# Order and pairing of the DFT pieces in an adaLN block with an S4D convolution and a token MLP

## The chip, the cores and the metric

The kernel runs on one core of a Trainium2 chip. A core has five engines with a row of instructions each: TensorE (PE, with its weight loads as PEld), VectorE (DVE), ScalarE (ACT), GpSimd (POOL) and SyncE (SP), which here only issues DMAs. The metric is the device time of the core in microseconds, lower is better; of several runs the median counts.

## The reference

An adaLN block over x of 2048 tokens by 448 channels. Six vectors (sa, ca, ga, sb, cb, gb) come from a small condition vector c. All in 32-bit floats:

```python
h = _layernorm(x, axis=-1) * (1 + ca) + sa
x = x + ga * _A_ref(h, ...)
h = _layernorm(x, axis=-1) * (1 + cb) + sb
x = x + gb * _B_ref(h, ...)
```

`_A_ref` is an S4D convolution along the tokens. Its kernel is a sum of 256 complex exponentials per channel, and the convolution goes through an FFT of twice the length:

```python
P = jnp.exp((A * dt[:, None])[:, :, None] * pos[None, None, :])
K = 2.0 * jnp.einsum("dn,dnl->dl", C, P).real
y = jnp.fft.irfft(Uf * Kf[None, :, :], L2)[:, :, :L]
```

`_B_ref` is a layer norm and a two-layer MLP with gelu over the tokens (2048 to 1792 to 2048), shared by the channels.

## The kernel before, in words

**Kernel generation.** The 448 channels go through in 28 groups of 16, each in two halves of 128 exponentials: 56 steps s. Eight steps make a batch. At its start stands a *window* (`window`), in which ScalarE computes magnitudes with the exponential table (L612); then come eight steps with the sine table. A step consists of: the phase product xe, xg on PE for the next step (L601, `st_phase`); six activations on ScalarE (L642 to L647); the two products G on GpSimd (L649, L650); the four products E on VectorE (L651 to L655); 64 small matmuls kg of the step before on PE (L676, `st_kgen`); and every second step a copy ks by ScalarE (L690). The tiles of the phase product are free for the next one when E has read them. Every four steps PE forms y from two groups (L714, `st_s1`), which is the first stage of the DFT of K; two PSUM buffers go to it, and ScalarE copies them to yk (L720).

**Pieces.** The convolution is done in a two-stage DFT. Its second stage is cut into 32 pieces of 224 columns: pieces 0 to 15 are the first half of the channels, 16 to 31 the second. A piece n consists of:
- `pc_load`: a load of u, the transformed input (224 KB), on SP (L739), and for n below 16 of its DFT tables si;
- `pc_s2`: the forward product kx, 8 matmuls on PE (L770) into one buffer of the PSUM pool `pms` (three buffers, shared with y and, for n below 16, with vv);
- `pc_mul`: the products zx and zy with u on VectorE (L778), and two sums z on engines that the caller names (L780, L781);
- `pc_tables`: for n above 16 the second table bt, made of the first by a negated and a plain copy (L759, L760); it has three buffers;
- `pc_inv`: the way back vv, 8 matmuls on PE (L795), two PSUM buffers; for n of 16 and above out of a pool of four, `pxs`;
- `pc_out`: two copies vt by ScalarE (L801) and a store to v_d in DRAM on SP (L803).

The tables of the first half are kept in the buffer yks[0], which its data no longer need (`pc_keep`, L750).

From step 33 on the first 16 pieces are woven into the generation steps by `piece`. It is called once a step (L1111), and in a window at three of its eight places. A call with `go` loads, issues kx and puts `pc_mul` into the list `dve`; where a piece was open before, it issues its way back and puts `pc_out` into the list `act`. These lists are emptied in the next step at fixed places (`flush`): `dve` between the second and third product E, `act` after the six activations. In the steps, `go` holds at odd s; at even s the call only brings the way back.

**Last stage.** When all of K is there, the pieces 16 to 31 run in one loop: in each turn load and kx of piece n, its products, one sum on GpSimd and one on VectorE, bt of piece n+1, and the way back of piece n-2. Then the token MLP: it reads v_d back as vt (L1198), makes the second stage of the way back as y (L1218), normalizes, and multiplies (acc, L1190 to L1192; o, L1324 to L1326). Its weights come through `WeightStream` with three raw buffers of 448 KB (L182); xt are rows of x (L1134, `x_pair`).

**What sets the order.** On PE, ACT, DVE and POOL the order is that in which the code is written. On SP a scheduler sets it, but for sections entered with `manual_schedule` for SP: in the last stage from the turn of piece 28 on (`last`). There the first w and the first xt go out in the turn of piece 29, and the second w after the loop.

Of the kernel before, what the change touches and what calls it, by code (L numbers as in the profile page):

```python
# [11 lines left out]
F32 = mybir.dt.float32  # L12
F32R = mybir.dt.float32r
BF16 = mybir.dt.bfloat16
AF = mybir.ActivationFunctionType
ALU = mybir.AluOpType
# [6 lines left out]
P = 128  # L23
# [193 lines left out]
def tile_adaln_s4d_mixer(ctx, tc, i, out):  # L217
# [20 lines left out]
    with ExitStack() as es:  # L238
# [496 lines left out]
        def pc_load(n):  # L735
            c, p = divmod(n, NP)
            u = fp.tile([P, 2, DC], F32, tag="u", name="u", bufs=4)
            rows = us_d[c, 2 * p : 2 * p + 2].rearrange("k (q c) d -> (k q) (c d)", c=2)
            nc.sync.dma_start(u.rearrange("p c d -> p (c d)"), rows)  # L739
            if c:  # L740
                w = kept(p)
            else:
                w = fp.tile([P, 4 * P], F32, tag="si", name="si", bufs=4)
                nc.sync.dma_start(w, si[:, p])
            pl[n] = u, w
            pt[n] = w[:, 2 * P : 3 * P], None if c else w[:, 3 * P : 4 * P]
# [5 lines left out]
        def pc_tables(n):  # L752

            real, h = pt[n][0], P // 2
            if n == NP:
                pt[n] = real, t0[:, 1]
                return
            imag = fp.tile([P, P], F32, tag="bt", name="bt", bufs=3)
            G.tensor_scalar(imag[:, 0:h], real[:, h:P], -1.0, None, ALU.mult)  # L759
            G.tensor_copy(imag[:, h:P], real[:, 0:h])  # L760
            pt[n] = real, imag

        def pc_s2(n):
            c, p = divmod(n, NP)
            k1 = yks[c][:, 2 * p : 2 * p + 2]
            pk[n] = pms.tile([P, 2, DC], F32, tag="ms", name="kx")
            for a in range(2):
                for k in range(2):
                    m = k * P + a * P // 2
                    T.matmul(  # L770
                        pk[n][64 * k : 64 * k + 64, a], pl[n][1][:, m : m + 64], k1[:, k], start=True, stop=True
                    )

        def pc_mul(n, e0, e1):
            u = pl.pop(n)[0]
            x, y, z = (fp.tile([P, 2, DC], F32, tag=t, name=t, bufs=b) for t, b in (("zx", 2), ("zy", 2), ("z", 3)))
            for j, t in enumerate((x, y)):
                V.tensor_tensor(t, pk[n], u[:, j : j + 1].to_broadcast([P, 2, DC]), ALU.mult)  # L778
            pk.pop(n)
            e0.tensor_tensor(z[:, 0], x[:, 0], y[:, 1], ALU.subtract)  # L780
            e1.tensor_tensor(z[:, 1], x[:, 1], y[:, 0], ALU.add)  # L781
            pz[n] = z, y

        def pc_inv(n):
            c, p = divmod(n, NP)
            pv[n] = [(pxs if c else pms).tile([P, DC], F32, tag="ms", name="vv") for _ in range(2)]
            z, y = pz.pop(n)
            terms = [(t, z[:, j], 2) for j, t in enumerate(pt.pop(n))]
            if p == 0:
                terms.append((t0[:, 0], y[:, 1], 1))  # L790
            for j, (t, zz, ks) in enumerate(terms):
                for k in range(ks):
                    r = slice(64 * k, 64 * k + 64)
                    last = j == len(terms) - 1 or (k == 1 and j == 1)
                    T.matmul(pv[n][k], t[r], zz[r], start=j == 0, stop=last)  # L795
# [150 lines left out]
                if k is not None:  # L946
                    f(k)

        def piece(go, eng=None):

            due = pieces[1] < pieces[0]
            if go:
                n = pieces[0]
                if n + 3 < 2 * NP:
                    pc_load(n + 3)
                pc_s2(n)
                if n:
                    pc_keep(n - 1)
                dve.append(partial(pc_mul, n, eng or G, eng or G))
                pieces[0] += 1  # L960
            if due:
                n = pieces[1]
                pc_inv(n)
                act.append(partial(pc_out, n))
                pieces[1] += 1
# [67 lines left out]
        for s in range(tail):  # L1033
            if s == 32:
                early.close()
                fp = es.enter_context(tc.tile_pool(name="fp", bufs=2, reuse_waits="tile"))
                m2p.append(right("m2l", BATCH - 3))
                yks[1] = fp.tile([P, 32, DC], F32, name="yk1", bufs=1)
                for n in range(3):
                    pc_load(n)  # L1040
                t0 = fp.tile([P, 2, P], F32, name="t0", bufs=1)
                nc.sync.dma_start(t0, i["T0"].rearrange("p (j m) -> p j m", j=2))
            if s % 2 == 0 and 0 < s and s // 2 + 2 < NG:
                load(s // 2 + 2, False)
            if s == 8:
                first.close()
            if s in late:
                late[s]()
            if s < NHALF and s % BATCH == 0:
                window(s)  # L1050
                if s == 0:
                    gp_ = right("gp", 3)
            if s % BATCH == 4:
                for g in range(s // 2 + 2, min(s // 2 + 6, NG)):
                    load(g, True)

            def between():
                flush(dve)
                if 2 <= s < BATCH:
                    for r in range(2 * s, 2 * s + 2):  # L1060
                        u_stats(r)
                if s < len(pace):
                    more(pace[s])

            mellow()
            if s >= NHALF:
                flush(dve)
                mellow()
            else:
                if s < 32 and s % BATCH > 1:  # L1070
                    st_kgen(s - 2)
                if (s + 1) % BATCH:
                    st_phase(s + 1)
                elif s + 1 < NHALF:
                    st_exponents(s + 1)

                if s > 32 and s % BATCH:
                    st_kgen(s - 1)
                st_step(s, between)
            flush(act)  # L1080
            if s == NHALF:
                st_kgen(s - 1)


            if s < 2:
                x_load(4 + 4 * s, 4 + 4 * s, G)
            free = s > 7 and not st_s1(s % BATCH == BATCH - 1)
            if s + 2 < 32 and (s + 2) % BATCH > 1:
                st_mag2(s + 2)

            if 1 < s < 8:
                modulation(s // 2, s % 2)
            if s == 7:
                par_load(2)

            if 8 <= s < 16 and free:
                some(u_rows, rows, 2 if s % 2 else 3)
            if s == 12:
                par_load(3)
            if s == 16:  # L1100
                spec.close()
                up = early.enter_context(tc.tile_pool(name="up", bufs=3, reuse_waits="tile"))
                for n in range(4):
                    u_load(n)
            if 17 <= s < 32 and free:
                some(u_cols, cols, 2 if s < 24 else 3)
            if s == 31:
                flush(dve)
                flush(act)
            if s > 32:  # L1110
                piece(pieces[0] < NP and (s % 2 == 1 or s >= NHALF))  # L1111
            if s == 34:

                for t in (ft, b1, b2):
                    V.memset(t, 0.0)
                nc.sync.dma_start(ft, i["FT"])
                nc.sync.dma_start(b1, i["B_b1"].rearrange("(t p) -> p t", p=P))
                nc.sync.dma_start(b2, i["B_b2"].rearrange("(t p) -> p t", p=P))
# [13 lines left out]
        def x_pair(r):  # L1132
            for g in range(2):
                nc.sync.dma_start(  # L1134
                    xts[r // 2][64 * g : 64 * g + 64].rearrange("p r d -> p (r d)"), token_pair(x, r, g)
                )
# [1 line left out]
        swp = es.enter_context(tc.tile_pool(name="swp", bufs=2, reuse_waits="tile"))  # L1138
        pc_keep(NP - 1)
        pc_tables(NP)  # L1140
        for k in range(NP + 2):

            n = NP + k
            if k < NP:
                if n + 3 < 2 * NP:
                    pc_load(n + 3)
                pc_s2(n)
                pc_mul(n, G, V)
            if k + 1 < NP:
                pc_tables(n + 1)  # L1150
            if k > 1:
                pc_inv(n - 2)
                pc_out(n - 2)
            if k == NP - 4:
                last = ExitStack()
                last.enter_context(tc.manual_schedule(engines={ENG.SP}))

            if k == NP - 3:
                wst.load()
                x_pair(0)  # L1160

        wst.load()
        last.close()

        S.activation(eps_t, eps_t, AF.Sqrt)
# [192 lines left out]
```

## Time and profile before

| what | value |
|---|---|
| median of 3 runs | 725.6 us (722.94 to 727.5) |
| profiled execution | 724.45 us, span of the core 722.7 us |
| mean granted PE clock | 0.939 |
| PE busy | 627.9 us, 87% |
| DVE busy | 460.3 us, 64% |
| ACT busy | 438.7 us, 61% |
| POOL busy | 273.2 us, 38% |
| DMA moved | 121.20 MB, mean 168 GB/s |

The span has these stages: kernel generation to about 384 us, the last stage of pieces to about 416, a seam to 425, and the MLP to the end. Busy shares are means over stages that differ, so each stage is read by itself. Names in the rows are those of the code (out<-in); numbers such as L795 are lines of the listing above. A bracket at the end of a row names the idle time ahead of the instruction and what ended it.

### The profile page before, as it was taken

The page shows a single profiled execution, that of the slowest core. Times are in us where ns is not written, and L with a number is a line of the kernel's source. Part 1 is how long each engine was busy: PE and PEld are TensorE (multiplying, and loading weights), DVE is VectorE, ACT ScalarE, POOL GpSimd, SP SyncE. Part 2 cuts the span into 40 slices and gives each one's busy share as a digit, 9 for nine tenths or more (in the row PEclk, how much of TensorE's full clock was granted, in tenths as well). Part 3 has the DMA queues.
Part 4 walks back from the last instruction along what each step waited for, and adds up shares of the span by engine and source line. Part 5 has one row for each costly group of instructions (what it writes and reads, how often), then busy time and mean ns, then how long its engine had stood idle before and what let it go on. Part 6 is the DMA issues. An engine that isn't in the chain of part 4 may idle for free. (4 is left out here: it accounts for less than half of the span.)

```text
span 722.7 us, 18269 instructions
## 1 busy us (share of the span) xinstructions
PE 627.9 (87%) x7204; PEld 449.9 (62%) x7204; DVE 460.3 (64%) x891; ACT 438.7 (61%) x849; POOL 273.2 (38%) x342
## 2 busy tenths in 40 slices
PE   0769899969988877888778939999999999999997
PEld 0335344535535545555455607777999999999996
DVE  7579779689779667575776738777722263333441
ACT  5848578887988888979862339778622242222220
POOL 6487438438648867977865600000000000000000
PEclk9988857988999989899999969999999999999999
DMA  6795364277888644444325899993585436655540
GB/s 169 207 189 144 144 195 136 112 234 197 236 225 251 212 84 144 127 128 122 96 82 164 233 274 248 237 224 100 169 230 166 141 99 173 176 164 154 153 140 27
DMA packets 101636, 121.20 MB, mean 168 GB/s; under 512 B 13066, under 2 KB 87422, under 8 KB 101422
## 3 DMA queue, kind: packets, MB, share of 16 engines
q1 hardware_dynamic: 100014, 113.16, 55.4%
q0 software_dynamic: 1536, 6.87, 4.2%
q8 instruction: 57, 0.93, 0.6%
q14 instruction: 29, 0.24, 0.1%
HBM read 84.64 MB, written 34.87 MB: 165 GB/s over the span
## 5 line engine op out<-in xcount | busy, mean ns | idle before, releaser
L202 ACT CAST whi<-w 128x896 fp32r<-128x896 f32 x64 | 59.8, 938 | 135.2 <-PE o L1325 84.7
L649 POOL TENSOR_TENSOR G<-mag,gs 128x512 f32<-128x512 f32 x56 | 71.8, 1282 | 86.5 <-ACT gs L645 86.3
L211 DVE TENSOR_TENSOR wlo<-w,whi 128x896 fp32r<-128x896 f32 x64 | 68.1, 1087 | 43.9 <-ACT whi L202 31.5
L601 PE MATMUL xg<-tab,lph 64*128 64x512 f32 x112 | 68.3, 612 | 21.3 <-ACT xg L647 7.1
L1190 PE MATMUL acc<-h3h,whi 128*128 128x448 f32 x224 | 83.6, 373 | 0.1
L1191 PE MATMUL acc<-h3l,whi 128*128 128x448 f32 x224 | 82.1, 367 | 0.0
L1192 PE MATMUL acc<-h3h,wlo 128*128 128x448 f32 x224 | 81.3, 363 | 0.0
L1325 PE MATMUL o<-ul,whi 128*128 128x448 f32 x224 | 81.3, 363 | 0.0
L1324 PE MATMUL o<-uh,whi 128*128 128x448 f32 x224 | 81.2, 362 | 0.0
L1326 PE MATMUL o<-uh,wlo 128*128 128x448 f32 x224 | 80.6, 360 | 0.0
L601 PE MATMUL xe<-tab,lph 64*128 64x512 f32 x112 | 67.8, 607 | 12.4 <-ACT gs L646 7.0
L676 PEld LDWEIGHTS kg<-E,G 128*32 128x32 f32 x3584 | 57.9, 117 | 29.6 <-issue 14.9
L650 POOL TENSOR_TENSOR G<-mag,gs 128x512 f32<-128x512 f32 x56 | 71.6, 1279 | 0.0
L676 PE MATMUL kg<-E,G 128*32 128x64 f32 x3584 | 67.7, 231 | 1.2 <-POOL G L649 0.5
L651 DVE TENSOR_TENSOR E<-m,xe 128x512 f32<-128x512 f32 x56 | 38.3, 683 | 38.2 <-ACT xe L644 29.8
L1328 DVE SCALAR_TENSOR_TENSOR y<-o,b,mod 128x448 f32<-128x448 f32 x16 | 10.9, 684 | 80.2 <-PE o L1326 80.2
L630 POOL TENSOR_TENSOR m<-mag,w 128x512 f32<-128x512 f32 x56 | 59.8, 1067 | 5.8 <-DVE E L655 1.5
L642 ACT ACTIVATE ab<-xe 128x512 f32<-128x512 f32 x56 | 33.9, 605 | 29.2 <-PE xe L601 17.9
L1190 PEld LDWEIGHTS acc<-h3h,whi 128*128 128x128 f32 x224 | 42.5, 190 | 13.9 <-ACT h L1246 7.0
L601 PE MATMUL xe<-tab,lex 64*128 64x512 f32 x56 | 30.4, 557 | 18.4 <-POOL wm L832 16.7
L612 ACT ACTIVATE mag<-xe 128x512 f32<-128x512 f32 x56 | 34.6, 619 | 16.5 <-PE xg L601 10.3
L1192 PEld LDWEIGHTS acc<-h3h,wlo 128*128 128x128 f32 x224 | 42.3, 189 | 3.0
(231 smaller groups left out, 1467.1 us busy)
## 6 DMA issues: line engine op xcount, KB each, us to landing
w<-in_B_w_dram SPq DMA_DIRECT2D x64, 224.0 KB
w<-in_B_w_dram SPq DMA_DIRECT2D x32, 448.0 KB
yu_d<-yt SPq DMA_DIRECT2D x16, 448.0 KB
yi<-yu_d SPq DMA_DIRECT2D x32, 224.0 KB
us_d<-uo SPq DMA_DIRECT2D x16, 448.0 KB
u<-us_d SPq DMA_DIRECT2D x32, 224.0 KB
v_d<-vt SPq DMA_DIRECT2D x32, 224.0 KB
vt<-v_d SPq DMA_DIRECT2D x16, 448.0 KB
```

The source lines that it names most:

```text
L202: self.nc.scalar.copy(hi, w)
L211: eng.tensor_tensor(lo, w, hi.bitcast(F32), ALU.subtract)
L601: T.matmul(out[k], lhs[r], rhs[r], start=start, stop=stop)
L649: G.tensor_tensor(Gt[:, 1], mg_, v32(sg), ALU.mult)
L650: G.tensor_tensor(Gt[:, 0], mg_, v32(cg_), ALU.mult)
L676: T.matmul(kgs[g][32 * q : 32 * q + 32, m], Gt[:, c, d], E[:, c, d], start=h == 0 and c == 0 and m == 0, stop=h == 1 and c == 1, skip_grou ...
L1190: nc.tensor.matmul(acc[f], hi[:, fs], h3h[:, r], start=r == 0, stop=False)
L1191: nc.tensor.matmul(acc[f], hi[:, fs], h3l[:, r], start=False, stop=False)
L1192: nc.tensor.matmul(acc[f], lo[:, fs], h3h[:, r], start=False, stop=r == 15)
L1324: nc.tensor.matmul(o, hi[:, ks], uh[kh][:, k], start=kh == 0 and k == 0, stop=False)
L1325: nc.tensor.matmul(o, hi[:, ks], ul[kh][:, k], start=False, stop=False)
L1326: nc.tensor.matmul(o, lo[:, ks], uh[kh][:, k], start=False, stop=kh == 1 and k == 6)
```

## The change

Four things are changed. The two copies that make bt move from GpSimd to ScalarE. The tiles z have two buffers instead of three for pieces 0 to 15, and four of another pool for the others. In the steps of the generation, the way back is no longer issued at even s but at odd s, behind the kx of the next piece; in windows it stays, and from s = 56 on, a call brings both as before. The last stage runs in pairs: both loads and both kx, then both products with both sums on GpSimd, then the way back of the two pieces of the pair before; the manual order of SP begins at pieces 24 and 25, two w are issued there and in the next pair, and xt in the pair of 28 and 29.

```diff
@@ pc_tables
-            G.tensor_scalar(imag[:, 0:h], real[:, h:P], -1.0, None, ALU.mult)
-            G.tensor_copy(imag[:, h:P], real[:, 0:h])
+            S.activation(imag[:, 0:h], real[:, h:P], AF.Copy, scale=-1.0)
+            S.copy(imag[:, h:P], real[:, 0:h])
@@ pc_mul
-            x, y, z = (fp.tile([P, 2, DC], F32, tag=t, name=t, bufs=b) for t, b in (("zx", 2), ("zy", 2), ("z", 3)))
+            x, y = (fp.tile([P, 2, DC], F32, tag=t, name=t) for t in ("zx", "zy"))
+            z = (fp if n < NP else swp).tile([P, 2, DC], F32, tag="z", name="z", bufs=2 if n < NP else 4)
@@ piece
-        def piece(go, eng=None):
-            due = pieces[1] < pieces[0]
+        def piece(go, eng=None, back=True):
+            due = pieces[1] < pieces[0] and back
@@ the steps
-                piece(pieces[0] < NP and (s % 2 == 1 or s >= NHALF))
+                go = pieces[0] < NP and (s % 2 == 1 or s >= NHALF)
+                piece(go, None, go or s >= NHALF)
@@ the last stage
-        for k in range(NP + 2):
-            n = NP + k
-            if k < NP:
-                if n + 3 < 2 * NP:
-                    pc_load(n + 3)
-                pc_s2(n)
-                pc_mul(n, G, V)
-            if k + 1 < NP:
-                pc_tables(n + 1)
-            if k > 1:
-                pc_inv(n - 2)
-                pc_out(n - 2)
-            if k == NP - 4:
+        for m in range(NP, 2 * NP + 2, 2):
+            if m < 2 * NP:
+                for n in (m, m + 1):
+                    if n + 3 < 2 * NP:
+                        pc_load(n + 3)
+                    pc_s2(n)
+                for n in (m, m + 1):
+                    pc_mul(n, G, G)
+                    if n + 1 < 2 * NP:
+                        pc_tables(n + 1)
+            if m > NP:
+                for n in (m - 2, m - 1):
+                    pc_inv(n)
+                for n in (m - 2, m - 1):
+                    pc_out(n)
+            if m == 2 * NP - 8:
                 last = ExitStack()
                 last.enter_context(tc.manual_schedule(engines={ENG.SP}))
-            if k == NP - 3:
+            if 2 * NP - 8 <= m < 2 * NP - 4:
                 wst.load()
+            if m == 2 * NP - 4:
                 x_pair(0)
-        wst.load()
         last.close()
```

On PE, at the end of a batch (the last matmuls of y, then the products xe and xg for the next window's magnitudes, kg of the last step, kx and vv of two pieces), the order before was:

```order
L714 MATMUL y_5047<-wc,ks 64x32x2
L714 MATMUL y_5048<-wc,ks 64x32x2
L795 MATMUL vv<-z,si 128x224 x4
L601 MATMUL xe<-tab,lex_145 128x512
L601 MATMUL xg<-tab,lex_145 128x512
L676 MATMUL kg<-E,G 32x64 x32
L770 MATMUL kx<-yk_1142,si 64x224 x4
L601 MATMUL xe<-tab,lex_145 128x512
```

and with the change it is:

```order
L714 MATMUL y_5047<-wc,ks 64x32x2
L714 MATMUL y_5048<-wc,ks 64x32x2
L601 MATMUL xe<-tab,lex_145 128x512
L601 MATMUL xg<-tab,lex_145 128x512
L676 MATMUL kg<-E,G 32x64 x32
L770 MATMUL kx<-yk_1142,si 64x224 x4
L796 MATMUL vv<-z,si 128x224 x4
L601 MATMUL xe<-tab,lex_145 128x512
```

The way back has moved from behind y to behind the next kx; all else keeps its place.

On SP, at the end of the last stage (loads of u, stores of v_d, weights w, rows xt, and the first loads of vt for the MLP), the order before was:

```order
L739 DMA u<-us_d 128x448
L803 DMA v_d<-vt 128x2x224 x3
L182 DMA w<-in_B_w_dram 64x1x896 x2
L1134 DMA xt_6070<-in_A_u_dram 64x1x896 x2
L803 DMA v_d<-vt 128x2x224 x4
L182 DMA w<-in_B_w_dram 64x1x896 x2
L1198 DMA vt<-v_d 128x2x448 x2
```

and with the change, from the two stores that end the first half (pieces 14 and 15) on:

```order
L804 DMA v_d<-vt 128x2x224 x2
L182 DMA w<-in_B_w_dram 64x1x896 x2
L739 DMA u<-us_d 128x448 x4
```

```order
L739 DMA u<-us_d 128x448
L804 DMA v_d<-vt 128x2x224 x2
L182 DMA w<-in_B_w_dram 64x1x896 x2
L739 DMA u<-us_d 128x448
L804 DMA v_d<-vt 128x2x224 x2
L1136 DMA xt_6070<-in_A_u_dram 64x1x896 x2
L804 DMA v_d<-vt 128x2x224 x4
L1202 DMA vt<-v_d 128x2x448 x2
```

The first w has moved ahead of the loads of u of the last stage; the second stands behind the stores of pieces 24 and 25, and the load of u for piece 31 behind it. Between the last stores and the first load of vt there is no w any more.

## The prediction

> **What bounds the kernel now.** I read the stages in a table of windows, then the chain of waits at the seam between them, then the waits of the stages that the change touches. Windows: from:to, length, busy time of PE, PEld, DVE, ACT and POOL, granted clock, DMA share, GB/s. The first is one batch of eight steps of the kernel generation, the second the last stage (pieces 16 to 31), the third the seam to the MLP, the fourth the MLP.
>
> ```profile
> 285.70:330.50 44.80, 36.91 (x812) 23.95 (x806) 30.08 (x50) 40.10 (x83) 35.33 (x40) 0.92 0.42 123
> 384.50:416.40 31.90, 29.92 (x258) 19.25 (x258) 24.59 (x48) 9.51 (x32) 20.33 (x46) 1.00 0.71 199
> 416.40:424.90 8.50, 0.04 (x2) 0.05 (x2) 2.24 (x3) 3.25 (x5) 0.00 (x0) 0.71 0.87 270
> 440.00:719.00 279.00, 278.37 (x1374) 249.59 (x1372) 137.73 (x269) 110.79 (x186) 0.00 (x0) 1.00 0.60 162
> ```
>
> ACT leads a batch (40.10 of 44.80), PE the last stage (29.92 of 31.90) and all of the MLP, which the change leaves alone. In the seam no engine works; the chain of waits shows two transfers there, the last piece's write and the read that follows it:
>
> ```profile
> 416.43 4.42 DMA v_d<-vt
> ...
> 420.97 3.85 DMA vt<-v_d
> ```
>
> So a gain must come from ACT's waits in a batch, from PE's pace in the last stage, or from the landing of the last v_d. The waits of 244 to 382 us (who waits, for whom: sum, times, longest):
>
> ```profile
> ACT ks L690 <- PE kg L676: 14.2, 10, 2.8
> ...
> PE vv L795 <- POOL z L780: 7.6, 8, 1.9
> ...
> PE vv L795 <- ACT yk L720: 5.9, 3, 2.0
> ```
>
> PE stands in front of vv, the product of the way back, for 13.5 us, and ACT stands for PE's kg. Whether the first causes the second has to be followed in one batch.
>
> **Generation stage.** The end of the batch that closes at 330.5 (start, length, engine, operation; in brackets the idle time before it):
>
> ```profile
> 318.04 0.68 DVE L655 TENSOR_TENSOR E<-m,xg 128x512 f32<-128x512 f32 x1
> ```
> ```profile
> 318.87 1.27 PE L795 MATMUL vv<-z,si 64*128 64x224 f32 x8 [1.89 <-POOL z L780]
> 319.81 0.55 PE L601 MATMUL xe<-tab,lph 64*128 64x512 f32 x1
> ...
> 324.02 1.10 PE L676 MATMUL kg<-E,G 128*32 128x64 f32 x64
> ...
> 329.12 0.65 PE L795 MATMUL vv<-z,si 64*128 64x224 f32 x4 [1.98 <-ACT yk L720]
> ```
> ```profile
> 320.31 0.62 ACT L801 COPY vt<-vv 128x224 f32<-128x224 f32 x2
> 321.13 0.60 ACT L642 ACTIVATE ab<-xe 128x512 f32<-128x512 f32 x1 [0.20 <-PE xg L601]
> ...
> 325.19 0.38 ACT L690 COPY ks<-kg 128x256 f32<-128x256 f32 x1 [0.97 <-PE kg L676]
> ...
> 329.85 0.68 ACT L801 COPY vt<-vv 128x224 f32<-128x224 f32 x2 [0.29 <-PE vv L795]
> 330.54 1.28 ACT L612 ACT_TABLE_LOAD   x1
> ```
>
> The vv at 318.87 leaves its place; it now follows the next step's kx. The stall of 1.89 does not go with it: next in PE's row is the phase product (L601), which needs the E that ends at 318.04 + 0.68 = 318.72. It starts at 318.7 instead of 319.81. From there to the first activation of that step it is 321.13 - 319.81 = 1.32, so it could start at 320.0; ACT is free at 320.31, the vt copies no longer being in between. The step starts 0.8 earlier. The second of ACT's waits, the 0.97 for kg, mostly stays: PE still does phase, kg, kx, vv, phase, kg in a row. Before, the row without vv took 324.02 + 1.10 - 319.81 = 5.31 us; vv adds 319.81 - 318.87 = 0.94, so kg ends at 318.7 + 6.25 = 324.95 instead of 325.12, and ks is 0.15 earlier. At the end of the batch vt waits no longer for vv before the table load: 330.54 - 329.85 = 0.69 and the 0.29 ahead of it, less the copies inside the next window, where they take about the 0.62 of the row at 320.31, though its ACT has no wait left to hide them. That leaves 0.15 + 0.98 - 0.62 = 0.5 a batch. If PE closes its switches better in the new row, the 0.8 reaches the end of the batch too and it is 1.2; if kg stays the only bound it is 0. I take 0.6 (nearest to the replay of rows), for two batches **-1.2**, from 0 to -2.4. Behind the moved wait on PE, where vv now may wait for z, stand the next phase product and kg; z has ended a step earlier there, so nothing is queued up by it.
>
> The third batch runs into the end of the stage:
>
> ```profile
> 348.31 1.93 PE L676 MATMUL kg<-E,G 128*32 128x64 f32 x64 [0.35 <-POOL G L650]
> ...
> 373.47 1.02 PE L795 MATMUL vv<-z,si 64*128 64x224 f32 x6 [1.99 <-ACT yk L720]
> ...
> 376.36 1.10 PE L676 MATMUL kg<-E,G 128*32 128x64 f32 x64
> ...
> 384.54 2.49 PE L770 MATMUL kx<-yk,yk 128*64 128x224 f32 x24 [1.17 <-ACT yk L720]
> ```
> ```profile
> 373.79 0.67 DVE L655 TENSOR_TENSOR E<-m,xg 128x512 f32<-128x512 f32 x1
> ```
>
> At 373.47 vv waited 1.99 us for two PSUM buffers that y holds until ACT has copied it, and kg, kx and the last kg stood behind it. Now kg and kx go first, into that stall; the kx needs only the third buffer. The last kg then waits for E, 373.79 + 0.67 = 374.46, instead of starting at 376.36: 1.9 earlier. Everything up to the last stage's first kx at 384.54 hangs on that kg and on that kx (copy, y, copy), so it comes along: **-1.9**, between -1.0 (if vv, now behind kx, holds kg up by its own 0.94) and -2.0 (the whole wait). The 0.35 wait for G goes or stays: **-0.2**. Stage: -3.3, from -1.0 to -4.8.
>
> **Last stage, PE.** The pace now and the parts:
>
> ```profile
> 394.70 0.98 PE L770 MATMUL kx<-yk,yk 128*64 128x224 f32 x8
> ...
> 396.56 0.98 PE L770 MATMUL kx<-yk,yk 128*64 128x224 f32 x8
> ...
> 413.25 0.55 PE L795 MATMUL vv<-z,yk 64*128 64x224 f32 x4
> 413.63 0.55 PE L795 MATMUL vv<-z,bt 64*128 64x224 f32 x4
> ```
>
> A piece takes 396.56 - 394.70 = 1.86. Run on end, 24 kx take 2.49 and 8 take 0.98, so 8 more cost 1.51 / 2 = 0.755; four vv cost 413.63 - 413.25 = 0.38, eight 0.76. That is 1.515; the other 0.35 are the two switches between kx (128*64) and vv (64*128). A pair makes two switches for two pieces: 3.03 + 0.35 = 3.38, that is 1.69 a piece. Five pairs in the middle gain 5 x 0.34 = 1.7, the first four kx on end and the last four vv on end some 1.1 more: -2.8, if nothing else is late. What could be (instructions of one tile: shortest/median/longest in ns, first and last start; the fourth row gives a group's busy us and mean ns):
>
> ```profile
> L780 POOL TENSOR_TENSOR z<-zx,zy x16: 763/792/797, 386.9 to 413.9; 128x224 f32<-128x224 f32 x16
> ```
> ```profile
> L780 POOL TENSOR_TENSOR z<-zx,zy x4: 657/658/662, 362.5 to 379.8; 128x224 f32<-128x224 f32 x4
> ```
> ```profile
> L781 DVE TENSOR_TENSOR z<-zx,zy x16: 391/392/393, 386.8 to 413.8; 128x224 f32<-128x224 f32 x16
> ```
> ```profile
> L801 ACT COPY vt<-vv 128x224 f32<-128x224 f32 x32 | 9.5, 349 | 22.4 <-issue 11.5 <-PE vv L795 9.8 <-ACT vt L801 1.1
> ```
>
> All four sums of a pair are now on GpSimd: 4 x 0.66 = 2.64 as where both sums stood on it (second row), 4 x 0.79 = 3.16 as beside DVE's sum (first row). I take 0.66, since DVE's sums are gone; both fit into 3.38, and bt no longer stands in between. The Trainium skill, "GPSIMD Engine Reference", section 4.1 "Engine selection", speaks against this edit: a two-input elementwise operation belongs on VectorE, being about twice as slow on GpSimd. By DVE's 0.39 in this stage (in the page's terms 0.78 on GpSimd) a pair would take 3.1 us there and the sum would stand; the 0.66 that this trace has for the same sum is 1.7 times, a little better than the rule. The bt tables on ACT are not in this trace: at most a vt copy each (0.349, which is three times as wide), 4 x 0.349 = 1.4 a pair, at least nothing; with 4 vt copies (1.4) ACT has 2.8 of 3.38. I take 1.0 for bt, and no wait.
>
> **Last stage, SP and DMA.**
>
> ```profile
> 410.83 2.11 SPq L182 DMA_DIRECT2D w<-in_B_w_dram  x2
> 413.04 1.19 SPq L1134 DMA_DIRECT2D xt<-in_A_u_dram  x2
> 414.32 2.62 SPq L803 DMA_DIRECT2D v_d<-vt  x4
> ```
> ```profile
> 400.00:412.00 12.00, 12.00 (x106) 7.42 (x106) 10.07 (x21) 3.95 (x14) 8.08 (x20) 1.00 0.81 247
> 414.00:420.00 6.00, 1.20 (x10) 0.68 (x8) 1.29 (x3) 3.58 (x8) 0.66 (x1) 0.99 1.05 300
> ```
>
> At a pace of 1.69 the share of 0.81 becomes 0.81 x 1.86 / 1.69 = 0.89, under the 1.05 that the queue has reached: PE stays the bound, if closely. But the load of u for piece 31 now stands on SP behind the stores of pieces 24 and 25 and behind the second w. Counted from the first kx of the stage, that of piece 26 starts at 16.0, vv of 25 ends at 19.2, its copy at 20.2, two stores (2.62 / 4 each) and w (2.11) are issued by 23.6, and u is there, between half of and all of the 4.42 of the last v_d, at 25.8 to 28. It is needed at 25.0, when kx of 31 is done. Some 2 us late: DVE waits for u, then GpSimd's sums, PE's last vv and the last vt hang on it. So the last v_d is issued not 2.8 but 0.7 earlier. It lands faster: the w that now goes out first, in the idle DMA time before the stage, is 1.5 us of transfer (0.46 MB at the 300 GB/s of 414 to 420) that no longer crowds the end; I take 0.6 of it. Last stage and seam: **-1.3**, from +0.3 (u at 28) to -4.3 (u on time and the whole 1.5).
>
> The z buffers (three to two, then four) cost nothing: in the generation stage z is read one step later, with two the third sum would wait only for a vv that is done by then; the cover is a step of some 4 us (the activations that begin at 321.13 end ahead of the ks copy at 325.19).
>
> **The rivals.** *Everything on time*: u lands before 25.0. For it: the DMA is not full between the pairs (0.81); against it: SP's order. Then 2.8 + 0.6: 724.45 - 3.3 - 3.4 = 717.7. Chance 0.20. *No gain in the generation stage*: the kg chain on PE takes back the 1.2 and the end gives only 1.0; for it speaks that ks waits 14.2 us for kg, mostly not because of vv. 724.45 - 1.0 - 1.3 = 722.1, or 723 with u late. Chance 0.22. *GpSimd becomes the bound of the last stage*, which ends slower than before: it decides from 3.38 / 4 = 0.85 us a sum, and from 3.72 / 4 = 0.93 it is slower than today's pace. Such a sum exists beside the other engine:
>
> ```profile
> 294.56 1.24 DVE L781 TENSOR_TENSOR z<-zx,zy 128x224 f32<-128x224 f32 x1
> ```
>
> That is DVE held up by GpSimd; if the sums, now beside DVE's products, took the same, a pair would take 4.96, 7.5 pairs (4.96 - 3.72) x 7.5 = 9.3 more: 724.45 - 3.3 + 9.3 = 730.5. Against it: the products have one operand in PSUM, and the sums beside such ones took 0.66. Chance 0.08. *The clock*: PE has a patch at half clock in this stage,
>
> ```profile
> 298.00:302.00 4.00, 1.14 (x4) 0.29 (x2) 2.57 (x4) 3.99 (x10) 3.84 (x6) 0.81 0.36 110
> 302.00:307.40 5.40, 5.38 (x79) 3.41 (x79) 3.85 (x6) 5.21 (x11) 5.02 (x5) 0.51 0.16 53
> ```
>
> after 4 us with 1.14 of PE's work; it costs 5.4 x (1 - 0.51) = 2.65 us of PE. Where PE's idle time moves, a patch can come or go: 717.1 or 722.4. Chance 0.08. By the Trainium skill, "TensorE: Matmul & The Clock Gate", Part 1, the clock halves after an idle window of about 3.4 us that runs freely; the rows agree in length (4.0 us, nearly idle), and by that rule it would be chance which batch is hit. *Not what it says*: "in other steps" puts the first w ahead of the whole last stage, not into the step in which it is written; it costs nothing there, and is in the sum.
>
> **How the numbers follow.** Forecast: -3.3 - 1.3 = -4.6, chance 0.42. The profiled execution took 724.45, so 719.9 by it; the median of the runs is 725.6, which gives 721.0. I say 720.2, own range 718 to 722.5. The range 716 to 726 takes in the first two rivals and the clock, and leaves out GpSimd's case and what lies beyond the ends. One per cent, about what a measurement of this kernel can tell, is 7.3 us: faster needs 718.3. There lie most of the first rival (0.14), half the clock's (0.04) and the forecast's edge (0.06): 0.24. Slower by that needs 732.9, which only GpSimd's case with a worse sum reaches: 0.05.
>
> **What would show it.** Right: PE's wait of 1.9 before vv is gone and a wait for E of 1.8 stands before the phase product; the last kg of the stage starts right behind E; kx comes in groups of 16 at 3.4 us a pair; GpSimd's sums are 0.66; a wait of DVE for u before piece 31. Wrong: sums over 0.85, ACT's waits at ks grown, ACT waiting with bt, vv of the last stage waiting for vt, or a last v_d that takes longer than 4.4 to land.

## The result and the profile after

| | before | with the change |
|---|---|---|
| median of 20 runs each | 728.54 us (722.94 to 734.16) | 720.07 us (715.54 to 724.03) |
| profiled execution | 724.45 us, span 722.7 | 723.32 us, span 721.5 |
| mean granted PE clock in it | 0.939 | 0.924 |

The ratio is 0.9875, with a 95% interval from 0.9851 to 0.9900: 9.1 us faster (7.3 to 10.9); the two medians themselves differ by 8.5. The two profiled executions differ by 1.1 us only, since that of before is quicker than its median and that of after slower. That hides most of the gain, and what hides it lies ahead of the change: the exponential table load of the third last batch starts 5.8 us later with the change, after code that is the same. From that landmark on, the two can be compared. ACT of both kernels, timeline (start, length, engine, line, operation; L612 is the load of the exponential table, L644 that of the sine table); first before, then after:

```profile
239.64 1.28 ACT L612 ACT_TABLE_LOAD   x1
...
285.74 1.28 ACT L612 ACT_TABLE_LOAD   x1
...
297.22 1.28 ACT L644 ACT_TABLE_LOAD   x1
...
330.54 1.28 ACT L612 ACT_TABLE_LOAD   x1
```

```profile
245.41 1.28 ACT L612 ACT_TABLE_LOAD   x1
...
289.19 1.28 ACT L612 ACT_TABLE_LOAD   x1
...
301.00 1.28 ACT L644 ACT_TABLE_LOAD   x1
...
333.07 1.28 ACT L612 ACT_TABLE_LOAD   x1
```

The first batch went from 46.10 to 43.78 us, the second from 44.80 to 43.88. PE, the first kx of the last stage (in before at 384.54) and the first y of the MLP; before, then after:

```profile
424.86 1.76 PE L1218 MATMUL y<-vt,ft 128*64 128x448 f32 x4 [9.12 <-DMA vt<-v_d]
```

```profile
384.83 3.36 PE L770 MATMUL kx<-yk,yk 128*64 128x224 f32 x32 [1.17 <-ACT yk L720]
...
423.64 1.76 PE L1222 MATMUL y<-vt,ft 128*64 128x448 f32 x4 [7.94 <-DMA vt<-v_d]
```

So the last batch with the end of the generation stage went from 54.00 to 51.76, the last stage with the seam from 40.32 to 38.81, and from there to the end both take 297.9. That is -2.3, -0.9, -2.2 and -1.5: 7.0 us, of which 5.5 in the generation stage.

The end of the batch that the prediction followed; first the ks of before that stands one ahead of its row of 325.19, then ACT and PE with the change:

```profile
317.05 0.37 ACT L690 COPY ks<-kg 128x256 f32<-128x256 f32 x1 [0.44 <-PE kg L676]
```

```profile
320.34 0.61 ACT L802 COPY vt<-vv 128x224 f32<-128x224 f32 x2
321.26 0.37 ACT L690 COPY ks<-kg 128x256 f32<-128x256 f32 x1 [0.32 <-PE kg L676]
...
324.66 0.60 ACT L642 ACTIVATE ab<-xe 128x512 f32<-128x512 f32 x1
...
328.69 0.37 ACT L690 COPY ks<-kg 128x256 f32<-128x256 f32 x1 [0.42 <-PE kg L676]
...
331.96 1.09 ACT L720 COPY yk<-y 128x512 f32<-128x512 f32 x2
```

```profile
321.13 0.50 PE L601 MATMUL xe<-tab,lph 64*128 64x512 f32 x1
322.65 0.46 PE L601 MATMUL xg<-tab,lph 64*128 64x512 f32 x1 [1.02 <-ACT gs L643]
...
323.72 1.10 PE L676 MATMUL kg<-E,G 128*32 128x64 f32 x64
324.75 0.98 PE L770 MATMUL kx<-yk,si 128*64 128x224 f32 x8
325.66 1.03 PE L796 MATMUL vv<-z,si 64*128 64x224 f32 x8
326.36 0.56 PE L601 MATMUL xe<-tab,lph 64*128 64x512 f32 x1
```

From ks to the next ks it takes 328.69 - 321.26 = 7.43 us (before 325.19 - 317.05 = 8.14), and from there to the table load 4.38 (before 5.35). ACT waits 0.42 for kg where it waited 0.97. The waits of 245 to 385 us say the same for the stage (who waits, for whom: sum, times, longest; in before, whose stage starts 5.8 earlier, the rows of the prediction are of 244 to 382):

```profile
ACT ks L690 <- PE kg L676: 9.4, 11, 2.9
...
PE vv L796 <- POOL z L781: 1.2, 1, 1.2
...
PE vv L796 <- ACT yk L720: 0.4, 1, 0.4
```

PE's 13.5 us in front of vv are 1.6 now, and ACT's 14.2 for kg are 9.4.

The last stage of after: pairs of kx on PE, one wait on VectorE, and GpSimd's sums:

```profile
390.30 1.73 PE L770 MATMUL kx<-yk,yk 128*64 128x224 f32 x16
...
394.33 1.74 PE L770 MATMUL kx<-yk,yk 128*64 128x224 f32 x16
...
397.71 1.73 PE L770 MATMUL kx<-yk,yk 128*64 128x224 f32 x16
```

```profile
411.93 0.62 DVE L779 TENSOR_TENSOR zx<-kx,u 128x448 f32<-128x448 f32 x1 [1.84 <-DMA u<-us_d]
```

```profile
L781 POOL TENSOR_TENSOR z<-zx,zy x16: 656/663/667, 387.2 to 413.3; 128x224 f32<-128x224 f32 x16
```

```profile
416.39 1.27 DMA v_d<-vt
```

```profile
416.38 1.28 ACT L1169 ACT_TABLE_LOAD   x1
```

```profile
419.71 1.23 SPq L1202 DMA_DIRECT2D vt<-v_d  x2
```

A pair takes 397.71 - 394.33 = 3.38 as forecast, and a sum 0.66; the pair ahead of it takes 4.03, and the last products wait 1.84 for u of piece 31. The last three rows are of the chain of waits, of ACT and of SP. The chain follows the last store, issued at 416.39, for 1.27 us only, but that is where ACT's table load ends (416.38 + 1.28 = 417.66), and not where the store lands; the 1.3 us that some expectations below name is this row. What the MLP waits for is the read, which SP issues when the store has landed: 419.71 - 416.39 = 3.32 us after it, before 420.97 - 416.43 = 4.54.

### The profile page after: what moved, and what is told of

Same layout as the page of the kernel before. It is cut to its first block, busy times and chain, and to the rows that moved or that the text cites. A ratio compares the mean times of both kernels' runs of the same rounds, so it can differ in the third digit from the quotient of the medians.

```text
span 721.5 us, 18291 instructions
## 1 busy us (share of the span) xinstructions
PE 630.4 (87%) x7204; PEld 455.2 (63%) x7204; DVE 453.3 (63%) x875; ACT 442.9 (61%) x879; POOL 273.4 (38%) x328
## 5 line engine op out<-in xcount | busy, mean ns | idle before, releaser
L676 PEld LDWEIGHTS kg<-E,G 128*32 128x32 f32 x3584 | 60.7, 121 | 32.5 <-issue 19.4
L676 PE MATMUL kg<-E,G 128*32 128x64 f32 x3584 | 70.8, 237 | 3.1 <-issue 2.3
L1332 DVE SCALAR_TENSOR_TENSOR y<-o,b,mod 128x448 f32<-128x448 f32 x16 | 10.9, 684 | 80.3 <-PE o L1330 80.3
L601 PEld LDWEIGHTS xg<-tab,lph 64*128 64x128 f32 x112 | 24.0, 214 | 37.1 <-issue 9.8
L612 ACT ACTIVATE mag<-xe 128x512 f32<-128x512 f32 x56 | 35.5, 634 | 17.8 <-PE xg L601 11.1
```

What stands on the lines that cost most here:

```text
L601: T.matmul(out[k], lhs[r], rhs[r], start=start, stop=stop)
L676: T.matmul(kgs[g][32 * q : 32 * q + 32, m], Gt[:, c, d], E[:, c, d], start=h == 0 and c == 0 and m == 0, stop=h == 1 and c == 1, skip_grou ...
```

## The experiments

Landmarks as above, in each traced execution (us); "old" marks a part that is as in the kernel before. The first three columns run from one exponential table load to the next, and from the last of them to the first kx of the last stage; the fourth from there to the first y.

| kernel | third last batch | second last | last and end | last stage, seam | ratio to before (95%) |
|---|---|---|---|---|---|
| before | 46.10 old | 44.80 old | 54.00 old | 40.32 old | |
| the change | 43.78 | 43.88 | 51.76 | 38.81 | 0.9875 (0.9851 to 0.9900) |
| back_only | 46.82 | 42.60 | 52.61 | 39.81 old | 0.9877 (0.9825 to 0.9928) |
| last_only | 45.44 old | 44.35 old | 54.03 old | 37.00 | 0.9947 (0.9904 to 0.9990) |
| end_only | 48.71 old | 47.11 old | 52.34 | 37.66 | 0.9967 (0.9931 to 1.0002) |
| back_ahead | 45.26 | 43.48 | 56.69 | 39.51 | 1.0002 (0.9969 to 1.0035) |
| z_two | 48.41 old | 44.91 old | 53.94 old | 40.09 old | 1.0042 (1.0004 to 1.0080) |
| w_behind_u | 43.75 | 43.85 | 51.74 | 38.35 | 0.9938 (0.9907 to 0.9969) |
| sums_split | 46.20 | 42.59 | 52.61 | 37.08 | 0.9871 (0.9819 to 0.9922) |
| loads_early | 44.20 | 42.59 | 52.60 | 37.12 | 0.9869 (0.9819 to 0.9919) |
| early_split | 43.86 | 43.90 | 51.77 | 37.64 | 0.9854 (0.9800 to 0.9907) |
| bt_pool | 43.75 | 43.77 | 51.70 | 37.99 | 0.9826 (0.9753 to 0.9899) |
| w_as_before | 43.84 | 43.89 | 51.76 | 38.17 | 0.9897 (0.9833 to 0.9960) |
| no_u | 44.15 | 43.71 | 51.66 | 36.87 | 0.9824 (0.9768 to 0.9880) |

**Which part brings it.** back_only is the kernel before with the change's `piece` and its call; last_only is the change with `piece(go)` in the steps:

```diff
-                piece(go, None, go or s >= NHALF)
+                piece(go)
```

> Only the way back of the generation steps moves (odd steps, behind kx); the last stage, its sums, tables and weight loads are those of before. Theory (the two parts add up, most of it in the generation stage): from the exponential table load of the third last batch to the first kx of the last stage the trace has 139.4 us, as with the whole change, against 144.9 before, give or take 1.5 for half-clock patches; the last stage and the seam stay at 40.3; 4.5 to 6 us faster than before. Rival (the gain is in the last stage, the batches only had luck with the clock patches): at most 2 us faster, and the ks copies still wait 0.9 us for kg at the end of a batch.

> Only the last stage is changed (pairs, both sums on GpSimd, bt on ScalarE, weight loads); the way back of the generation steps stays at the even steps. Theory: from the first kx of the last stage to the first y of the MLP 38.8 us, against 40.3 before; 1 to 2 us faster than before. Rival: the gain of the seam is worth more than the trace of one execution shows (weights that are there earlier let the MLP start at a higher clock or without a wait): 3 to 4 us faster.

The way back alone has a ratio as good as the whole change, the last stage alone 0.9947. In the trace back_only's generation stage takes 46.82 + 42.60 + 52.61 = 142.0 instead of the 139.4 expected (144.9 before); the third last batch had more half-clock time (10.5 us against 7.0 in before, counted in slices of half a us), which the gain of single traces must be read against. The rival that the gain lies in the last stage is out. last_only's 3.9 us are more than the 1 to 2 of its theory; its interval (0.7 to 7.0) holds both theory and rival. The two parts add up to 1.8%, more than the 1.25% of the whole change, though within their intervals.

**Where in the generation stage.** end_only keeps the even steps up to step 47; back_ahead puts the way back ahead of kx in `piece` (in all calls that bring both, those after step 55 too).

```diff
-                piece(go, None, go or s >= NHALF)
+                piece(go, None, go or s >= NHALF or s < 48)
```

> The whole change, but up to step 47 the way back stays at the even steps; only in the last batch it comes with the next kx. Theory (two batches gain 1.4 us each by steps that start earlier and a table load that no longer waits for vt; the third batch and the end of the stage gain 2): the two batches take 90 to 91 us together as before, from the third table load to the first kx of the last stage it takes 51.8 to 52.6 as with the change; the kernel is about 3 to 4 us slower than the whole change, half of its gain. Rival (the gain of the generation stage is at its end, the batches change only with the half-clock patches): as fast as the whole change within 1.5 us.

> The whole change, but in a call that brings both, the way back stands ahead of the next kx. Theory (in the batches it matters only that vv no longer waits for z right behind G; at the end of the stage, and after each y, it matters that kx stands ahead, because vv waits for the buffers that y holds): the batches take what they take with the change, 43.8 without a patch too many; from the third table load to the first kx of the last stage 53.5 to 54 instead of 51.8, PE waits about 2 us for the yk copies ahead of vv in step 55 again; 1 to 2.5 us slower than the whole change. Rival (the place behind kx is what helps everywhere): the batches too lose 0.5 to 1 each, 3 to 4 us slower.

end_only's two batches took 95.8 together, more than the 90 to 91 expected, and its end 52.34; with 0.9967 it lacks 6.7 us of the change, where 3 to 4 were expected. So the batches carry most of the gain. back_ahead's batches (45.26 and 43.48) are near those of the change, while its end took 56.69. The place behind kx matters little where y holds the buffers: there the two ks stand 6.95 apart, with the change 6.54. It matters, which the expectation had left out, in the last calls, where vv now stands in front of kx and waits for its z: from the last ks to the first kx of the last stage it takes 10.24 where the change takes 7.03. In these calls the kernel before, too, has vv behind kx, so this part is no test of the move itself. PE of back_ahead:

```profile
368.62 1.02 PE L796 MATMUL vv<-z,si 64*128 64x224 f32 x6 [1.16 <-ACT yk L720]
...
372.69 1.26 PE L796 MATMUL vv<-z,si 64*128 64x224 f32 x8 [1.11 <-POOL z L781]
...
377.00 1.26 PE L796 MATMUL vv<-z,si 64*128 64x224 f32 x8 [2.14 <-POOL z L781]
```

It is as slow as before, which is 9 us more than the change where 1 to 2.5 were expected; the trace shows some 5 of them (56.69 - 51.76), in an execution with a half-clock stretch more at the end (378 to 382). That execution (721.2 us) is the shortest of twelve, nine of which took 726 to 730; where the others lose the rest stays open.

**The buffers of z** alone, in the kernel before:

> The kernel before with the change's buffers for z alone (two for pieces 0 to 15, four of another pool for the rest). Theory: no difference, within 1 us; no wait of GpSimd for vv. Rival (the buffers are a part of the gain, by their place in memory or by what they let start earlier): 2 us faster or more.

No gain, and no wait of GpSimd for vv; the ratio is even 0.4% above 1. By themselves they are no part of the gain.

**Weights and u.** w_behind_u sends the second w with xt, in the pair of 28 and 29; w_as_before sends the first w there and the second after the loop.

```diff
-            if 2 * NP - 8 <= m < 2 * NP - 4:
+            if m == 2 * NP - 8:
                 wst.load()
             if m == 2 * NP - 4:
+                wst.load()
                 x_pair(0)
```

> The whole change, but the second w goes out behind the load of u for piece 31 (with xt, in the pair of pieces 28 and 29). Theory (u of piece 31 comes late because it stands behind the stores of 24 and 25 and behind that w): VectorE's wait of 1.84 us for u goes or falls under 0.7, the last vv comes 1.2 to 1.8 earlier, and 38.8 from the first kx to the first y becomes 37.3 to 38.0. Rival (the seam is paced by the DMA queues, whatever the order): the last store is issued earlier but lands as late, since w now runs beside the last stores; 38.8 give or take 0.4.

> The whole change, but the first w goes out in the pair of pieces 28 and 29 and the second after the last stores, as before. Theory (w that stand at the end crowd the last stores and the first read): no wait for u of piece 31, but the last store lands in 4 us or more instead of 1.3 to 2.8; 38 to 39.5 us from the first kx to the first y, 0.5 to 2 us slower than the change. Rival (where w stand is worth nothing, since they fill the gap of the seam either way): 37 to 38, no difference.

In both VectorE no longer waits for u of piece 31, and the last vv ends 28.6 us after the first kx instead of 30.9. But the seam takes it back. The chain of w_behind_u:

```profile
414.51 4.38 DMA v_d<-vt
...
419.04 3.87 DMA vt<-v_d
```

From the issue of the last store to that of the read it takes 419.04 - 414.51 = 4.53 us, as before the change; in after it took 3.32. The DMA share stays at 0.9 to 1.1 until 417.2 here, where in after the queues were empty at 416.25. 38.35 and 38.17 against 38.81 and, in other traces of the change's stage, 37.0 and 37.7: the stage is no shorter, as the rival of w_behind_u (the queues pace the seam) and the theory of w_as_before had it. The ratio of w_behind_u is 0.6% worse than that of the change, which its trace does not show; why stays open.

loads_early writes both w into the pairs of 18 and 20 and xt into that of 22, where the scheduler still sets SP's order; three of the four transfers of w go out from 376.67 on, ahead of the first kx:

> The whole change, but both w and the first xt go out at the beginning of the last stage, where the queues have room, none of them behind the stores of piece 24. Theory (the seam is paced by what the queues still have to move, and the last vv by u of piece 31): no wait of VectorE for u of piece 31, the last vv 1.5 us earlier, the last stores land within 2.5 us, and from the first kx to the first y it takes 35 to 36.5 us instead of 37.0 to 38.8; 1.5 to 3 us faster than the whole change. Rival (the first pairs then wait for u of pieces 19 and 20 behind these loads, or the MLP misses nothing of it): 37 us or more, no gain.

37.12, so its rival. The read follows the last store by 2.27 us (409.28 to 411.55), 1 us sooner than in after, but now early products wait for u (VectorE of loads_early):

```profile
398.28 0.62 DVE L779 TENSOR_TENSOR zx<-kx,u 128x448 f32<-128x448 f32 x1 [2.31 <-DMA u<-us_d]
```

no_u leaves out the loads of u from piece 20 on:

> The whole change, but pieces 20 to 31 load no u of their own and take that of pieces 16 to 19 (this part of the computation is left out): 2.75 MB less for the DMA queues in the last stage, all work of the engines as with the change. Theory (the seam is paced by what the queues have to move, and PE, which every reordering of loads has freed, only waits longer for the last read): the last vv ends 28.6 us after the first kx as with w behind u, the last store lands in 1.3 to 2.5 us, and the first y comes 34.0 to 35.5 us after the first kx, 2 us or more under all other variants. Rival (a fixed chain of last vt, store, its receipt and the read sets the seam, whatever the queues carry): 36.5 us or more.

36.87, so the theory's 34.0 to 35.5 was missed. The last vv ended at 28.6, but the read came late. From the chain of waits and from SP's timeline of no_u:

```profile
413.80 1.49 DMA v_d<-vt
```

```profile
417.55 1.23 SPq L1209 DMA_DIRECT2D vt<-v_d  x2
```

The 1.49 again ends on ACT, not with the store. The read is issued 417.55 - 413.80 = 3.75 us after the store, and the y of 421.36 starts 3.81 after the read. The number is that of the rival, its fixed chain is not: the second part is 3.7 to 4.0 in all traces, the first goes from 2.23 to 4.57 (2.27 in loads_early, 2.24 in last_only). Nor were the queues empty without u: the DMA share is 0.7 to 1.2 from 411.5 to 415.75. So 36.87 is no floor. An order with the last vt copy at 29.3, as here, and a read 2.27 after it would come to 29.3 + 2.3 + 3.9 = 35.5, an estimate from these rows; none was run.

**Sums and tables.** sums_split has `pc_mul(n, G, V)` in the pairs; bt_pool makes bt on GpSimd as before; early_split is sums_split with SP in the order of the code for the whole stage, w in the pairs of 16 and 18 and xt in that of 20.

> The whole change, but the second sum of each piece of the last stage is on VectorE, as before. Theory (GpSimd's sums do not bound the pairs, except at the beginning, where four kx come on end): sums on GpSimd take 0.79 instead of 0.66, a pair still takes 3.38 us; the second pair of the stage, which takes 4.03 with both sums on GpSimd, takes 3.4 to 3.6, and the stage is 0.3 to 0.9 us shorter. Rival (two sums on GpSimd are what makes the pairs possible, since VectorE must be free for the products): pairs of 3.6 us and more, the stage 1 to 2 us longer.

> The whole change, but the bt tables stay on GpSimd, as before. Theory (bt on ScalarE is what gives GpSimd room for both sums): GpSimd has 4 x 0.66 + 2 x 0.60 = 3.84 us a pair, over the 3.38 of PE, so pairs take 3.7 to 4.1 and the last stage is 2 to 4 us longer than with the whole change. Rival (there is slack, bt could have stayed): pairs of 3.4 us, no difference.

> The whole change, with the second sum of the last stage on VectorE, and both w and the first xt written out by hand behind the loads of u of the first three pairs (SP in the order of the code for the whole last stage). Theory (the last stage has three places where something is late: GpSimd's sums in the second pair, u of piece 31, and the queues at the end): no 4.0 us pair, no wait for u over 0.7, and 34.5 to 36.5 us from the first kx to the first y; 1 to 4 us faster than the whole change. Rival (what is gained at the front is lost to the queues): 37 us, as sums_split and loads_early each had.

With one sum on VectorE the 4.03 of that pair are 3.38 (PE of sums_split), though a sum on GpSimd takes longer (tile z of sums_split):

```profile
390.07 1.73 PE L770 MATMUL kx<-yk,yk 128*64 128x224 f32 x16
393.45 1.73 PE L770 MATMUL kx<-yk,yk 128*64 128x224 f32 x16
```

```profile
L781 POOL TENSOR_TENSOR z<-zx,zy x16: 770/776/869, 386.7 to 412.4; 128x224 f32<-128x224 f32 x16
```

So GpSimd bounded the change's stage at its beginning, as the theory had it, and the place of the second sum does not change the pace after that. With bt on GpSimd (PE of bt_pool) a pair takes 3.49, not 3.7 to 4.1:

```profile
401.00 1.73 PE L770 MATMUL kx<-yk,yk 128*64 128x224 f32 x16
404.49 1.73 PE L770 MATMUL kx<-yk,yk 128*64 128x224 f32 x16
```

GpSimd's instructions overlap a little: sums start 0.62 apart, and four of them with two tables cost 3.49. Moving bt to ScalarE is worth 0.11 us a pair. early_split fell to its rival: 37.64, with a wait of 2.1 us for u in the middle of the stage. None of these is told apart from the change by its ratio.

## Why the prediction was right, and where its sizes were not

**The time and the difference.** 720.2 was forecast and 720.07 measured; but the forecast was 4.6 us below the profiled execution of before, and the measured difference is 9.1. The two meet by luck, because the three runs shown (725.6) and the profiled one (724.45) lay below the 728.54 that 20 runs give. The signs and the places were right, the sum was half of what came.

**The batches (forecast -0.6 each; mis-sized).** The start of the step came nearly as forecast: vt no longer stands ahead of it. The sign that was named, a wait of 1.8 for E ahead of the phase product, did not come: its first half starts at 321.13 without a wait, and only its second half waits 1.02, for ACT, just behind the last E (321.87 + 0.68 = 322.55). The end came: 5.35 - 4.38 = 0.97 against 0.98. What failed is the replay of PE in between, "ks is 0.15 earlier": it is 8.14 - 7.43 = 0.71. The replay held the whole product back until E, but the second half alone waits; it starts 1.39 us after ks (322.65 - 321.26) where the whole product started 2.76 after it (319.81 - 317.05), 1.37 earlier and not 1.1. And vv behind kx costs 326.36 - 325.66 = 0.70, not the 0.94 that it took where it stood alone after a stall. The window, with vt copies now in it, is 0.33 longer (301.00 - 289.19 = 11.81 from one table load to the next, before 297.22 - 285.74 = 11.48), not 0.62. That makes -0.71 - 0.97 + 0.33 = -1.35 a batch.

These pieces hardly vary. In the second last batch the last two ks stand 7.43 to 7.45 apart in nine traces of the new order (without back_ahead) and 8.13 to 8.15 in four of the old; from the second of them to the table load it takes 4.37 to 4.38 in the new and 5.35 to 5.36 in the old. What varies is the rest of a batch, where half-clock stretches fall: in the batch shown it took 321.26 - 301.00 = 20.26, before 317.05 - 297.22 = 19.83, so that the batch gained 0.92 and not 1.35. In all traces of the table the old order takes 47.2 and 45.3 on average, the new one 44.5 and 43.4: -2.7 and -1.9, half-clock stretches included. Of the third last batch these are 11.3 us in the old order and 8.1 in the new, so the 2.7 is not all gain.

**Third batch and end (forecast -2.1): -2.24**, and 54.0 to 52.1 over all traces. The terms are not those of the forecast. ACT at the stall of vv behind y, in before and then in after, and PE of after:

```profile
369.54 0.37 ACT L690 COPY ks<-kg 128x256 f32<-128x256 f32 x1 [0.97 <-PE kg L676]
...
377.53 0.37 ACT L690 COPY ks<-kg 128x256 f32<-128x256 f32 x1 [2.65 <-PE kg L676]
```

```profile
371.26 0.37 ACT L690 COPY ks<-kg 128x256 f32<-128x256 f32 x1 [0.42 <-PE kg L676]
...
377.80 0.37 ACT L690 COPY ks<-kg 128x256 f32<-128x256 f32 x1 [0.71 <-PE kg L676]
```

```profile
375.29 1.41 PE L796 MATMUL vv<-z,si 64*128 64x224 f32 x8
376.63 1.10 PE L676 MATMUL kg<-E,G 128*32 128x64 f32 x64
```

vv does not wait for yk here any more, but it stands behind kx and holds the last kg up: E ends at 375.52 + 0.68 = 376.20, and kg starts when vv is through. The ks comes 6.54 after the one ahead of it and not 7.99, so the term is -1.45, between the -1.9 taken and the lower bound of -1.0. The step ahead of it gives 0.7 more, and the rest of the batch 0.1. The sum had no gain of the steps in this batch, so that -2.1 and -2.24 meet is partly luck.

**Last stage (forecast -1.3): -1.51** in after's trace, and 40.1 to 37.8 on average over after, last_only and end_only, which have the change's stage (back_ahead, with 39.51, is left out). The pace (3.38), the sums (0.66) and u of piece 31 (1.84 late, 2 forecast) were as written. The two terms of the seam were not. The last v_d was to be issued 0.7 earlier: it is 31.56 after the first kx (416.39 - 384.83), before 31.89, so 0.33; missing were the pair of 4.03, which waits for GpSimd (0.65), and a granted clock of 0.50 from 414.5 on, under the last vv. It was to land 0.6 faster: the read follows it in 3.32 instead of 4.54, so 1.22. The two misses cancel. In last_only and end_only, where the last vv runs at full clock, it is issued 1.0 earlier, and the read follows in 2.24 and 2.93. bt on ScalarE was costed at 1.0 a pair, and is 2 x (0.26 + 0.23) = 0.98 (tile bt of after):

```profile
L759 ACT ACTIVATE bt<-yk x15: 256/257/269, 384.7 to 410.6; 128x64 f32<-128x64 f32 x15
L760 ACT COPY bt<-yk x15: 227/228/245, 384.8 to 410.8; 128x64 f32<-128x64 f32 x15
```

With these averages, -2.7 - 1.9 - 1.9 - 2.3 = -8.8, which is the measured 9.1 within its interval.

**The rivals.** "Everything on time" could not have given its 717.7 by u alone: w_behind_u had u on time, and its stage was no shorter. "GpSimd becomes the bound" held for one pair. "No gain in the generation stage" is refuted by back_only. The clock moved single batches by 1 to 3 us, as its rival had it, with no sign of its own (its two times are 717.2 and 722.5 by its own terms).

## What to carry to other kernels

An operation that waits behind a slower producer should be put not only where its operand is ready, but where its output buffers are free and where the next urgent product does not queue behind it; whether it goes ahead of or behind a neighbour can be worth as much as the move itself (back_ahead lost all of it, in its trace mostly in the last calls, where the kernel before had the better order already). Moving a transfer off one wait helps only if the chain that ends last is not paced by the same queues: here the reorderings of the loads traded a wait for u against a later read of the last store, or against an earlier wait for u. And a row of a chain of waits ends with what was released next; whether that is the consumer in question has to be looked up on its own engine. Stages are compared from landmark to landmark, over several traces, not by two spans.

## What the runs showed of the hardware

PE's half-clock stretches, mostly 3.5 or 7 us each in slices of half a us, fall into different places of the generation stage from trace to trace (in before at 256 to 263, 300.5 to 307.5 and 348 to 351.5, in after at 247 to 250.5, 264 to 267.5, 305 to 312 and 349.5 to 353). The same code ahead of the third last batch took from 236.5 (back_only) to 245.4 us (after), and the second last batch of the same order from 42.6 to 43.9. The 20 runs of one kernel spread over 8 to 11 us, with granted clocks of 0.944 in the shortest run of after (715.54) and 0.923 in the longest (724.03); the order of two kernels within 0.5% is open here. That the old order also has more such stretches, because PE idles in it, was not shown: at like stretches the gain is still 0.9 (44.80 to 43.88, 7 us in both) to 2.4 us a batch (46.10 to 43.75 in w_behind_u, 7 us in both).

The last store lands with the last of the 16 DMA engines. Three windows of after (from:to, length, busy time of PE, PEld, DVE, ACT and POOL, granted clock, DMA share, GB/s):

```profile
417.50:418.00 0.50, 0.00 (x0) 0.00 (x0) 0.06 (x1) 0.49 (x3) 0.00 (x0) 0.50 0.93 317
...
418.50:419.00 0.50, 0.00 (x0) 0.00 (x0) 0.26 (x1) 0.50 (x2) 0.00 (x0) 0.50 0.06 20
419.00:419.50 0.50, 0.00 (x0) 0.00 (x0) 0.50 (x1) 0.50 (x1) 0.00 (x0) 0.50 0.00 0
```

By 418.0 nearly all of the 224 KB has moved; until 419.0 packets still move at a share of 0.06, as of one engine in sixteen, and SP issues the read 0.7 us later, at 419.71. In no_u the one engine is 1.2 us behind the others, in loads_early and last_only 0.1, and the reads follow the stores in 3.75, 2.27 and 2.24. Why that engine is late stays open.

From the last packet to the read that depends on the store it takes 0.5 to 0.7 us in the ten traces where no w runs behind the stores (0.57 in loads_early, 0.55 in no_u), but from where the other engines are through it takes 0.6 to 1.8. The Trainium skill, "DMA: Bandwidth & Descriptors", section "Anatomy of one DMA", has a fixed cost of about 2 us for a transfer, most of it the receipt of the write; it gives this for transfers that GpSimd issues. The stores here, issued by SP, do not bear that out: in loads_early the packets move for 0.9 of the 2.27 us from store to read, which leaves some 1.4, of which 0.6 lie behind the last packet.
